# Turning the row maxima of a sliding-window attention on VectorE instead of TensorE, with eight small DMAs per head pair

## The chip, the cores and the metric

The kernel runs on one core of one Trainium2 chip. The metric is the device time of one execution in microseconds (us), the median of the runs given. A difference of 0.2% or less can't be told from no change with this kernel.

## The reference

One transformer block with adaptive layer norm, in fp32: 2048 tokens, width 448, 16 heads of 28, a causal window of 256 keys, and a feed-forward of width 1792 with the Mish activation.

```python
mod = (_silu(c) @ w_mod).reshape(c.shape[0], 6, 1, -1)
sa, ca, ga, sb, cb, gb = (mod[:, i] for i in range(6))
h = _layernorm(x) * (1 + ca) + sa
q, k, v = split(h @ wqkv)                      # 16 heads of 28
scores = einsum("bhqd,bhkd->bhqk", q, k) * 28 ** -0.5
scores = where(0 <= iq - ik < 256, scores, -1e9)
x = x + ga * (softmax(scores) @ v) @ wo
h = _layernorm(x) * (1 + cb) + sb
x = x + gb * (mish(h @ w1 + b1) @ w2)
```

## The kernel before, in words

The tokens are cut into four groups of 512. A group's attention goes head by head, 64 heads over all (`NS`), and each head in three steps `u` (192 steps). A head's queries stand in a tile `q` of 86 rows by 512 tokens, its keys in `k` of 86 rows by 768. fp32 values are carried as a high and a low part, so a head's 28 dimensions take 84 rows. Rows 84 and 85 of `q` hold the high and the low part of each query's row maximum, and the same rows of `k` hold -1: the matmul that makes the scores for the exponential subtracts the maximum as it goes. Two heads share one `q` tile (a "pair", 32 over all); there are three such tiles.

A head passes these steps, and instructions stand in each engine's queue in the order in which the loop over `u` writes them:

- `L` loads `q` and `k` of a head, five heads ahead. Every DMA of this stretch is issued by SP (`dma`, line 59), in program order.
- `A` (lines 676 to 687), three heads ahead: for each of four blocks `t` of 128 queries TensorE makes 128 x 384 scores `sA`, and VectorE adds the mask and reduces them to a maximum per query, a column of `mx`.
- `M2` (lines 689 to 697), once a pair: carries the pair's maxima to the `q` tile. The maxima stand with the queries on 128 partitions (8 columns, head by block), and rows 84 and 85 want them along the free dimension of one partition. `M2` stands three steps `u` ahead of the pair's first `B`.
- `B` (line 713) makes the scores `sB` transposed, keys by queries, for one third of the head; ScalarE takes the exponential twice (`P`, `Ph`), GpSimd makes the low part `Pl`, and `PV` (line 745) multiplies by the values.

Between these, filler matmuls (the projections of the next group, the output projection of the last) are put on TensorE. After the attention comes the feed-forward. TensorE works its queue in order; a waiting `sB` holds whatever stands behind it.

The tile framework makes the waits: an instruction waits for semaphores of those that wrote what it reads. DMAs take turns on eight semaphores, `DMAHW0` to `DMAHW7`.

Of the kernel before, what the change touches and what calls it, by code (L numbers as in the profile page):

```python
# [8 lines left out]
F32 = mybir.dt.float32  # L9
F32R = mybir.dt.float32r  # L10
BF16 = mybir.dt.bfloat16
AF = mybir.ActivationFunctionType
ALU = mybir.AluOpType
# [7 lines left out]
NQ, NK, NV, LEAD = 6, 6, 10, 3  # L21
# [30 lines left out]
def adaln_block(ctx: ExitStack, tc: tile.TileContext, x, wqkv, wo, w1, b1, w2, c, w_mod, out):  # L52
    nc = tc.nc
    PE, ACT, DVE, POOL = nc.tensor, nc.scalar, nc.vector, nc.gpsimd
# [3 lines left out]
    def dma(o, i):  # L58
        nc.sync.dma_start(o, i)

    def pool(name, side="left", space=None):
        kw = {} if space is None else {"space": space}
        cm = tc.tile_pool(name=name, bufs=1, reuse_waits="tile", side=side, **kw)
        st = ExitStack()
        return st.enter_context(cm), st
# [26 lines left out]
    def bank(tag, bufs, name):  # L92
        return PS[0].tile([128, 512], F32, name=name, tag=tag, bufs=bufs)
# [18 lines left out]
    for k in range(4):  # L112
        wmf = st0.tile([128, 2 * D], F32, name=f"wm01_{k}")
        t = wmf[0:112]
# [11 lines left out]
    for part in range(3):  # L126
        for ci in range(4):
            r0, r1 = ci * 128, min(ci * 128 + 128, D)
            for h in ((slice(0, 128),) if ci < 3 else (slice(0, 64), slice(64, 128))):
                t = wqs[ci][h]  # L130
# [9 lines left out]
    ident = cst.tile([128, 128], F32, name="ident")  # L140
# [329 lines left out]
    Q2 = [kq.tile([86, 2, GT], F32R, name="q2_0")]  # L470
# [43 lines left out]
    att, att_s = pool("att")  # L514
# [5 lines left out]
    for i in range(2):  # L520
        t = att.tile([128, GT], F32, name=f"o2_{i}")
# [150 lines left out]
    NS = NG * H  # L672
    mx, Pt, Ph, Pl, pvb, et, olt = {}, {}, {}, {}, {}, {}, {}
    junk = att.tile([128, 384], F32, name="junk")

    def A(i, t):
        g, h = divmod(i, H)
        q, k = Q3[i % NQ], K3[i % NK]
        if i % 2 == 0 and t == 0:
            mx[i // 2] = att.tile([128, 2, 4], F32, name=f"mx{i}", tag="mx", bufs=2)  # L680
        c0 = max(256 - 128 * t, 0) if g == 0 else 0
        p = bank("sA", 2, f"sA{i}_{t}")
        PE.matmul(p[:, c0:384], q[0:84, t * 128:(t + 1) * 128], k[0:84, t * 128 + c0:t * 128 + 384],  # L683
                  start=True, stop=True)
        DVE.tensor_tensor_reduce(out=junk[:, c0:384], in0=p[:, c0:384], in1=mask[:, c0:384], scale=1.0,  # L685
                                 scalar=-3.0e38, op0=ALU.add, op1=ALU.max,
                                 accum_out=mx[i // 2][:, i % 2, t:t + 1])

    def M2(pr):
        p = bank("tr", 1, f"mt{pr}")  # L690
        PE.transpose(p[0:8, 0:128], mx[pr].rearrange("p a t -> p (a t)"), ident)
        r = att.tile([8, 2, 128], F32R, name=f"mr{pr}", tag="mr", bufs=2)
        DVE.tensor_copy(r[:, 0], p[0:8, 0:128])
        DVE.tensor_tensor(r[:, 1], p[0:8, 0:128], r[:, 0].bitcast(F32), op=ALU.subtract)
        for i in range(2):
            dma(Q2[pr % (NQ // 2)][84 + i:85 + i].bitcast(F32).rearrange("o a (t n) -> o (a t) n", t=4),
                r[:, i].bitcast(F32))

    def units(g, b):
        return [x for x in BLOCKS[b] if g > 0 or x[0] >= 2]  # L700
# [324 lines left out]
    for i in range(LEAD):  # L1025
        for t in range(4):
            A(i, t)
            fill0()
            side_step(0)
        if i % 2:  # L1030
            M2(i // 2)
            load_slot(LEAD + 1)
    NU = 3 * NS
    credit = 0.0
    for u in range(NU + 9):
# [14 lines left out]
        a = s + LEAD  # L1050
        if a < NS:
            A(a, (0, 1, 3)[k])
        if k == 0 and (a - 1) % 2 == 1 and LEAD <= a - 1 < NS:
            M2((a - 1) // 2)
        if k == s % 2 and s < NS:
            load_slot(s + LEAD + 2)
        if s % 2 == 1 and 1 <= (s - 1) // 2 <= NS // 2:
            pr = (s - 3) // 2
# [24 lines left out]
        if k == 1 and a < NS:  # L1083
            A(a, 2)
# [73 lines left out]
    for n in range(NN + 1):  # L1158
        g, f = divmod(n, NF)
# [47 lines left out]
```

## Time and profile before

| | before |
|---|---|
| median of 3 runs | 705.66 us (704.79 to 706.11) |
| span of the profiled execution, first to last instruction | 703.9 us |
| what the median has above that span | 1.76 us |
| TensorE clock granted | 1.000 |
| bytes read from and written to HBM | 56.60 MB and 32.51 MB |
| DMA engines' busy share of the span | 42.0% |
| attention with its fillers | 44 to 400 us |

How to read the profile: PE is TensorE, PEld its loading of weights, DVE VectorE, ACT ScalarE, POOL GpSimd and SP SyncE, which here only issues DMAs (SPq is its sequencer, and a row's duration there is the time of the issue, not of the transfer). A row of the timeline has the start and the duration in us, engine, line, operation, and out<-in; in brackets the idle time before it and what ended it. A row of a tile has the shortest, median and longest duration in ns. In a row of waits stand the sum in us, how many, and the longest. The mean in a row of groups is in ns, behind the busy us.

### The profile page before, as it was taken

Reading aid. Unit: us, or ns where it says so; the run is one execution under the profiler, and the core shown is the slowest. Engines: PE = TensorE matmul, PEld = TensorE weight load, DVE = VectorE, ACT = ScalarE, POOL = GpSimd, SP = SyncE. Lnnn points to the kernel's source line nnn. Section 1 sums busy time; section 2 is a strip of 40 time slices with the busy share of each in tenths; the row PEclk is TensorE's granted clock in tenths of the full one; section 3 lists DMA queues with packets and bytes.
Section 4 is the critical chain, followed back from the end, with each engine's and each line's share of the span. In section 5 each row is a group of like instructions: output and inputs, shape, how many; then the busy total and the mean of one; then the engine's idle time right before and its main releaser. Section 6 shows DMA issues by size and latency. Waiting matters only on the chain.

```text
span 703.9 us, 11999 instructions
## 1 busy us (share of the span) xinstructions
PE 685.9 (97%) x4001; PEld 590.2 (84%) x4001; DVE 383.3 (54%) x1030; ACT 391.6 (56%) x740; POOL 326.4 (46%) x355
## 2 busy tenths in 40 slices
PE   9899999999999999999999899999999999999997
PEld 8777888888888888898887788878888888888886
DVE  5688658788655887655768755452224222421112
ACT  3628788777667867667878974344233323332221
POOL 6626779686666776666778957212010000000000
PEclk9999999999999999999999999999999999999999
DMA  7865664455662462663773165800350035001001
GB/s 209 259 221 188 208 204 152 139 181 157 181 209 76 158 207 88 185 211 95 226 216 120 54 203 170 227 20 1 104 117 4 0 106 119 1 1 52 1 1 52
DMA packets 75178, 90.16 MB, mean 128 GB/s; under 512 B 31535, under 2 KB 51741, under 8 KB 75117
## 3 DMA queue, kind: packets, MB, share of 16 engines
q1 hardware_dynamic: 74652, 89.39, 42.0%
q8 instruction: 32, 0.52, 0.3%
q14 instruction: 30, 0.24, 0.1%
q10 hardware_dynamic: 464, 0.00, 0.0%
HBM read 56.60 MB, written 32.51 MB: 127 GB/s over the span
## 4 chain that ended last, share of the span: by engine, by line
PE 78%; DVE 6%; DMA 6%; ACT 3%; POOL 3%; issue 3%; SPq 1%; DVEq 0%; POOLq 0%; ACTq 0%
PE z L917 17%; PE pv L745 10%; PE qk L315 8%; PE sA L683 5%; PE acc L1106 5%; PE acc L1104 5%; PE acc L1105 5%; PE sB L713 5%; PE wo L315 4%; PE qk_v L315 4%; PE sB L724 3%; DMA scr<-st 2%; PE et L759 2%; PE warm L428 1%; DVE junk L685 1%
## 5 line engine op out<-in xcount | busy, mean ns | idle before, releaser
L735 POOL TENSOR_TENSOR Pl<-P,Ph 128x512 fp32r<-128x512 f32 (+2 forms) x192 | 234.8, 1230 | 80.9 <-ACT Ph L728 46.6
L685 DVE CUSTOM_DVE_ANT_0 junk<-sA,mask 128x384 f32<-128x384 f32 (+2 forms) x256 | 135.1, 528 | 95.1 <-PE sA L683 87.4
L727 ACT ACTIVATE P<-sB 128x512 f32<-128x512 f32 (+2 forms) x192 | 109.6, 571 | 62.3 <-PE sB L724 58.1
L925 DVE TENSOR_TENSOR al<-t,ah 128x512 fp32r<-128x512 f32 x56 | 39.2, 700 | 181.8 <-ACT ah L924 181.8
L923 ACT ACTIVATE t<-z,b1c 128x512 f32<-128x512 f32 x56 | 38.3, 684 | 138.6 <-PE z L917 138.6
L728 ACT ACTIVATE Ph<-sB 128x512 fp32r<-128x512 f32 (+2 forms) x192 | 109.2, 569 | 0.0
L683 PE MATMUL sA<-k,q 84*128 84x384 f32 (+2 forms) x256 | 100.5, 396 | 1.8 <-DVE mx L685 1.1
L917 PE MATMUL z<-hlf,w 128*128 128x512 f32 x224 | 88.6, 395 | 0.0
L917 PE MATMUL z<-hhf,w 128*128 128x512 f32 x224 | 88.6, 395 | 0.0
L1104 PE MATMUL acc<-w2h,ah 128*128 128x448 f32 x224 | 82.2, 367 | 1.2 <-ACT ah L924 1.2
L1106 PE MATMUL acc<-w2h,al 128*128 128x448 f32 x224 | 82.1, 366 | 0.1
L1105 PE MATMUL acc<-w2l,ah 128*128 128x448 f32 x224 | 81.6, 364 | 0.0
L745 PE MATMUL pv<-Ph,v 128*60 128x256 f32 (+2 forms) x352 | 76.7, 292 | 0.6 <-ACT o L751 0.5
L745 PE MATMUL pv<-Pl,v 128*60 128x256 f32 (+2 forms) x352 | 74.0, 284 | 2.4 <-POOL Pl L735 1.4
L713 PE MATMUL sB<-q,k 86*128 86x256 f32 (+1 forms) x352 | 74.2, 285 | 0.5 <-DMA q<-mr 0.5
L917 PE MATMUL z<-hhf,w1l 128*128 128x512 f32 x168 | 66.3, 395 | 0.0
L713 PEld LDWEIGHTS sB<-q,k 86*128 86x128 f32 x352 | 61.5, 189 | 2.3 <-DMA q<-mr 1.5
L724 PE MATMUL sB<-fdmask,identr 128*128 128x128 bf16 (+1 forms) x320 | 60.1, 253 | 0.0
L745 PEld LDWEIGHTS pv<-Ph,v 128*60 128x60 f32 x352 | 45.8, 133 | 14.0 <-ACT o L751 1.9
L745 PEld LDWEIGHTS pv<-Pl,v 128*60 128x60 f32 x352 | 45.2, 132 | 11.5 <-POOL Pl L735 3.8
L683 PEld LDWEIGHTS sA<-k,q 84*128 84x128 f32 x256 | 48.9, 193 | 7.0 <-DVE mx L685 4.3
L917 PEld LDWEIGHTS z<-hlf,w 128*128 128x128 f32 x224 | 42.2, 188 | 10.0
(159 smaller groups left out, 1252.4 us busy)
## 6 DMA issues: line engine op xcount, KB each, us to landing
scr<-st SPq DMA_DIRECT2D x24, 512.0 KB
k<-scr SPq DMA_DIRECT2D x48, 252.0 KB
q<-scr SPq DMA_DIRECT2D x64, 168.0 KB
scr<-st SPq DMA_DIRECT2D x32, 256.0 KB
x<-x1d SPq DMA_DIRECT2D x10, 448.0 KB
xin<-in_A_x_dram SPq DMA_DIRECT2D x8, 448.0 KB
xr<-in_A_x_dram SPq DMA_DIRECT2D x16, 224.0 KB
x1d<-xr SPq DMA_DIRECT2D x16, 224.0 KB
```

Of the source, the lines that this page charges most:

```text
L315: PE.matmul(p, b, a, start=(n == 0), stop=(n == 10))
L683: PE.matmul(p[:, c0:384], q[0:84, t * 128:(t + 1) * 128], k[0:84, t * 128 + c0:t * 128 + 384], start=True, stop=True)
L685: DVE.tensor_tensor_reduce(out=junk[:, c0:384], in0=p[:, c0:384], in1=mask[:, c0:384], scale=1.0, scalar=-3.0e38, op0=ALU.add, op1=ALU.max ...
L713: PE.matmul(p[:, c:c + 128 * (t1 - t0)], k[:, jj * 128:(jj + 1) * 128], q[:, t0 * 128:t1 * 128], start=(n == 0), stop=False, skip_group_ch ...
L727: ACT.activation(P[:, c0:], p[:, c0:], AF.Exp, scale=SCALE)
L728: ACT.activation(Ph[u][:, c0:], p[:, c0:], AF.Exp, scale=SCALE)
L735: eng.tensor_tensor(Pl[u][:, a:b], Pt[u][:, a:b], Ph[u][:, a:b].bitcast(F32), op=ALU.subtract)
L745: PE.matmul(pv[0:60, t0 * 128:t1 * 128], V[j % NV][:, h, :], P[u][:, c:c + 128 * (t1 - t0)], start=(P is Ph and b == 0 and n == 0), stop=F ...
L917: PE.matmul(zb[n], ps[m][1], ps[m][0], start=(m == 0), stop=(m == 10))
L1104: PE.matmul(p, ah[n][:, ts], w2h[f], start=(f == 0), stop=False)
L1105: PE.matmul(p, ah[n][:, ts], w2l[f], start=False, stop=False)
L1106: PE.matmul(p, al[n][:, ts], w2h[f], start=False, stop=(f == NF - 1))
```

## The change

Before, TensorE turns the 128 x 8 block of maxima to 8 x 128 in PSUM (`mt`), VectorE splits that in high and low part (`mr`, 8 partitions of 128 tokens each), and two DMAs, one for each part, carry 8 rows of 128 tokens to rows 84 and 85 of the pair's `q`. After, VectorE splits the maxima where they stand (8 columns high, 8 columns low, in the tile `mhl` of 32 columns), turns `mhl` in four blocks of 32 x 32 by one instruction, and finds in `mr`, for each block of 32 tokens, 8 partitions of high and 8 of low parts. Each part of each block goes by a DMA of its own: 2 x 4 of them, 8 rows of 32 tokens each. `mx` becomes a flat tile of 8 columns, and `mhl` is cleared once by GpSimd.

```diff
+    mhl = att.tile([128, 32], F32R, name="mhl")
+    POOL.memset(mhl.bitcast(F32), 0.0)
...
-            mx[i // 2] = att.tile([128, 2, 4], F32, name=f"mx{i}", tag="mx", bufs=2)
+            mx[i // 2] = att.tile([128, 8], F32, name=f"mx{i}", tag="mx", bufs=2)
...
     def M2(pr):
-        p = bank("tr", 1, f"mt{pr}")
-        PE.transpose(p[0:8, 0:128], mx[pr].rearrange("p a t -> p (a t)"), ident)
-        r = att.tile([8, 2, 128], F32R, name=f"mr{pr}", tag="mr", bufs=2)
-        DVE.tensor_copy(r[:, 0], p[0:8, 0:128])
-        DVE.tensor_tensor(r[:, 1], p[0:8, 0:128], r[:, 0].bitcast(F32), op=ALU.subtract)
+        DVE.tensor_copy(mhl[:, 0:8], mx[pr])
+        DVE.tensor_tensor(mhl[:, 8:16], mx[pr], mhl[:, 0:8].bitcast(F32), op=ALU.subtract)
+        r = att.tile([128, 32], F32, name=f"mr{pr}", tag="mr", bufs=2)
+        DVE.transpose(r, mhl.bitcast(F32))
         for i in range(2):
-            dma(Q2[pr % (NQ // 2)][84 + i:85 + i].bitcast(F32).rearrange("o a (t n) -> o (a t) n", t=4),
-                r[:, i].bitcast(F32))
+            rows = Q2[pr % (NQ // 2)][84 + i:85 + i].bitcast(F32).rearrange("o a (t n) -> o (a t) n", t=4)
+            for b in range(0, 128, 32):
+                dma(rows[:, :, b:b + 32], r[b + 8 * i:b + 8 * i + 8])
```

`M2` is called at the same place. What it moves shows in the engines' queues. SP near the end of the attention, before (`q<-mr` is a DMA of the maxima, `q<-scr` and `k<-scr` are loads of a head, `x1d<-xr` is a store):

```order
L59 DMA x1d<-xr_5261 128x448
L59 DMA q_2_460<-mr_5657 1x8x128 x2
L59 DMA q_1_459<-scr 84x512
L59 DMA k_2_146<-scr 84x768
L59 DMA x1d<-xr_5517 128x448
L59 DMA q_1_459<-scr 84x512
L59 DMA k_3_148<-scr 84x768
```

The same place on SP after the change:

```order
L59 DMA x1d<-xr_5398 128x448
L59 DMA q_2_460<-mr_5804 1x8x32 x8
L59 DMA q_1_459<-scr 84x512
L59 DMA k_2_146<-scr 84x768
L59 DMA x1d<-xr_5664 128x448
L59 DMA q_1_459<-scr 84x512
L59 DMA k_3_148<-scr 84x768
```

Nothing changes its place; six more issues stand ahead of the loads that follow. VectorE at a pair's `M2`, before (`ISA` is the masked reduction and the reading of its result into `mx`):

```order
L685 ISA junk,mx_4385<-sA_0_4386,mask 128x384
L685 ISA mx_4385 128x1
L693 CAST mr_4391<-mt_4389 8x128
L694 TENSOR_TENSOR mr_4391<-mt_4389,mr_4391 8x128
L175 SCALAR_TENSOR_TENSOR wm_0_4161<-wm_1_4191,sT,wm_0_4161 112x448
```

and after:

```order
L687 ISA junk,mx_4497<-sA_0_4498,mask 128x384
L687 ISA mx_4497 128x1
L692 CAST mhl<-mx_4315 128x8
L693 TENSOR_TENSOR mhl<-mx_4315,mhl 128x8
L695 STREAM_TRANSPOSE mr_4503<-mhl 128x32
L175 SCALAR_TENSOR_TENSOR wm_0_4268<-wm_1_4298,sT,wm_0_4268 112x448
```

Two instructions become three, in the same place behind the next pair's first reduction. TensorE from a pair's `M2` to the pair's first `sB`, before, with the semaphores that each row waits for (`L315` is filler):

```order
L683 MATMUL sA_0_2358<-k_0_142,q_0_377 128x384 [waits DMAHW7_49,DMAHW6_49,DVE_49]
L691 MATMUL mt_2361<-ident,mx_2168 8x128 [waits DVE_49]
L315 MATMUL wo_1_2333<-wol_472,hho_2111 128x448
...
L713 MATMUL sB_2449<-q_2_460,k_4_150 128x384 [waits DMAHW7_49,DMAHW0_49]
L713 MATMUL sB_2449<-q_2_460,k_4_150 128x128
```

and after:

```order
L685 MATMUL sA_0_2415<-k_0_142,q_0_377 128x384 [waits DMAHW1_49,DMAHW0_49,DVE_49]
L315 MATMUL wo_1_2390<-wol_472,hho_2163 128x448
L315 MATMUL wo_1_2390<-wo_1_468,hlo_2164 128x448
...
L715 MATMUL sB_2511<-q_2_460,k_4_150 128x384 [waits DMAHW4_49,DMAHW5_49,DMAHW3_49,DMAHW6_49,DMAHW2_49,DMAHW7_49,DMAHW1_49,DMAHW0_49]
L715 MATMUL sB_2511<-q_2_460,k_4_150 128x128
```

The transpose `mt` is gone, 32 times in all, and the first `sB` of a pair waits for all eight DMA semaphores in place of two.

More of the change, by code (lines that the diff above doesn't have):

```diff
@@ L686, in A @@
                                  scalar=-3.0e38, op0=ALU.add, op1=ALU.max,
-                                 accum_out=mx[i // 2][:, i % 2, t:t + 1])
+                                 accum_out=mx[i // 2][:, i % 2 * 4 + t:i % 2 * 4 + t + 1])
     def M2(pr):
-        p = bank("tr", 1, f"mt{pr}")
-        PE.transpose(p[0:8, 0:128], mx[pr].rearrange("p a t -> p (a t)"), ident)
-        r = att.tile([8, 2, 128], F32R, name=f"mr{pr}", tag="mr", bufs=2)
-        DVE.tensor_copy(r[:, 0], p[0:8, 0:128])
-        DVE.tensor_tensor(r[:, 1], p[0:8, 0:128], r[:, 0].bitcast(F32), op=ALU.subtract)
+        DVE.tensor_copy(mhl[:, 0:8], mx[pr])
+        DVE.tensor_tensor(mhl[:, 8:16], mx[pr], mhl[:, 0:8].bitcast(F32), op=ALU.subtract)
+        r = att.tile([128, 32], F32, name=f"mr{pr}", tag="mr", bufs=2)
+        DVE.transpose(r, mhl.bitcast(F32))
         for i in range(2):
-            dma(Q2[pr % (NQ // 2)][84 + i:85 + i].bitcast(F32).rearrange("o a (t n) -> o (a t) n", t=4),
-                r[:, i].bitcast(F32))
+            rows = Q2[pr % (NQ // 2)][84 + i:85 + i].bitcast(F32).rearrange("o a (t n) -> o (a t) n", t=4)
+            for b in range(0, 128, 32):
+                dma(rows[:, :, b:b + 32], r[b + 8 * i:b + 8 * i + 8])
     def units(g, b):
```

## The prediction

> **What bounds the kernel now.** I read the page first, then the stretch in which the changed code runs (44 to 400 us), then the rows of the tiles that the change touches.
>
> ```profile
> PE 685.9 (97%) x4001; PEld 590.2 (84%) x4001; DVE 383.3 (54%) x1030; ACT 391.6 (56%) x740; POOL 326.4 (46%) x355
> ...
> PEclk9999999999999999999999999999999999999999
> ...
> PE 78%; DVE 6%; DMA 6%; ACT 3%; POOL 3%; issue 3%; SPq 1%; DVEq 0%; POOLq 0%; ACTq 0%
> ```
>
> TensorE is busy 97% of the span at full clock, and 78% of the chain that ended last is TensorE's. By stage:
>
> ```profile
> 44.00:400.00 356.00, 348.52 (x2386) 299.09 (x2385) 254.21 (x793) 267.00 (x538) 256.29 (x242) 1.00 0.53 165
> ```
>
> In the attention stretch (columns: span, then PE, PEld, DVE, ACT, POOL busy) PE is busy 348.5 of 356 us; no other engine is over 267. So a new PE wait here counts in full, and a DVE instruction counts only if PE ends up waiting for it. The whole `mr` path today:
>
> ```profile
> L59 SPq DMA_DIRECT2D q<-mr x64: 625/640/1362, 44.8 to 396.4; - x64
> L693 DVE CAST mr<-mt x32: 272/274/279, 44.5 to 395.3; 8x128 fp32r<-8x128 f32 x32
> L694 DVE TENSOR_TENSOR mr<-mt,mr x32: 277/279/280, 44.8 to 395.7; 8x128 fp32r<-8x128 f32 x32
> ```
>
> The number to keep is 640 ns: SP spends that to issue one `q<-mr` DMA, and nothing else passes SP meanwhile. One head pair in order of time (pair 17 of 0 to 31):
>
> ```profile
> 229.66 0.42 PE L683 MATMUL sA<-k,q 84*128 84x384 f32 x1
> 229.92 0.27 PE L691 MATMUL mt<-ident,mx 128*8 128x128 f32 x1
> ...
> 230.12 0.56 DVE L685 CUSTOM_DVE_ANT_0 junk<-sA,mask 128x384 f32<-128x384 f32 x1
> ...
> 230.60 0.27 DVE L693 CAST mr<-mt 8x128 fp32r<-8x128 f32 x1
> ...
> 230.90 1.38 SPq L59 DMA_DIRECT2D q<-mr  x2
> 230.91 0.28 DVE L694 TENSOR_TENSOR mr<-mt,mr 8x128 fp32r<-8x128 f32 x1
> ```
> ```profile
> 235.57 0.37 PEld L713 LDWEIGHTS sB<-q,k 86*128 86x128 f32 x2
> ```
>
> The last row is the pair's first score tile, which reads rows 84 and 85 of `q` and so needs every `mr` DMA. From first issue to use: 235.57 - 230.90 = 4.67 us. I call this D. It differs from pair to pair; the first pair, the longest and the last:
>
> ```profile
> 44.83 2.17 SPq L59 DMA_DIRECT2D q<-mr  x2
> ...
> 48.23 0.19 PEld L713 LDWEIGHTS sB<-q,k 86*128 86x128 f32 x1 [0.80 <-DMA q<-mr]
> ```
> ```profile
> 204.46 1.51 SPq L59 DMA_DIRECT2D q<-mr  x2
> ```
> ```profile
> 210.57 0.36 PEld L713 LDWEIGHTS sB<-q,k 86*128 86x128 f32 x2
> ```
> ```profile
> 395.64 1.35 SPq L59 DMA_DIRECT2D q<-mr  x2
> ```
> ```profile
> 398.23 0.30 PEld L713 LDWEIGHTS sB<-q,k 86*128 86x128 f32 x2
> ```
>
> D is 3.40, 6.11 and 2.59 us; over all 32 pairs the same two rows give 3.98 on the mean. In the first pair PE already waited for the landing:
>
> ```profile
> 45.64 2.49 DMA q<-mr
> ```
> ```profile
> PEld sB L713 <- DMA q<-mr: 1.5, 3, 0.8
> ```
>
> The second DMA landed at 45.64 + 2.49 = 48.13, and SP had finished issuing at 44.83 + 2.17 = 47.00: landing comes 1.13 us after the last issue ends. Three such waits cost 1.5 us in the whole run; today the path just fits.
>
> **Part by part. The PE transposes (32, removed).** On the chain one of them takes:
>
> ```profile
> 52.73 0.11 PE mt L691
> ```
>
> 32 x 0.11 = 3.5 us of PE time. PE also waited for the maxima before some of them:
>
> ```profile
> PEld mt L691 <- DVE mx L685: 2.3, 3, 0.9
> ```
>
> That makes 5.8 us, the most this can give. But the transpose stands in the stretch between `M2` and the score tile. If that stretch ends in a wait for DMAs, PE merely arrives earlier at the wait, so in the forecast I count it as nothing.
>
> **DVE: two instructions become three.** Before, the first DMA went 0.30 us after the first of them began (230.60 to 230.90), beside the second. Now both DMA halves need the turned block. The nearest rows:
>
> ```profile
> L414 DVE TENSOR_SCALAR sT<-sT 112x4 f32<-112x4 f32 x1 | 0.1, 136 | 0.0
> ```
> ```profile
> L416 DVE TENSOR_TENSOR sT<-sT,cT 112x4 f32<-112x4 f32 x1 | 0.2, 164 | 0.0
> ```
> ```profile
> L1139 DVE STREAM_TRANSPOSE zt<-z 128x512 f32<-128x512 f32 x12 | 8.4, 704 | 0.0
> ```
> ```profile
> L685 DVE CUSTOM_DVE_ANT_0 junk<-sA,mask 128x384 f32<-128x384 f32 x224 | 123.9, 553 | 80.2 <-PE sA L683 76.1
> ...
> L685 DVE CUSTOM_DVE_ANT_0 junk<-sA,mask 128x128 f32<-128x128 f32 x16 | 4.6, 287 | 11.9 <-PE sA L683 8.5 <-issue 3.2
> ```
>
> 256 columns more cost 553 - 287 = 266 ns, 1.04 ns each, so a 32-column transpose should take about 704 - 480 x 1.04 = 205 ns (bounds 136 and 704). 0.14 + 0.16 + 0.21 = 0.51 us, then the issue: the first DMA goes 0.22 us later. DVE's total stays as it is (0.51 against 0.55 a pair). It no longer waits for PE here, but the row of line 685 above (230.12, just ahead of the cast) shows that the previous reduction, not the transpose, ended last; nothing is gained. The one POOL memset lies in the setup and costs nothing.
>
> **SP: two issues become eight.** Two take 1.38 us, so start to start is 0.74, and eight take 7 x 0.74 + 0.64 = 5.82 us. The new form, 8 pieces of 128 B for 8 of 512 B, isn't in the trace. Bounds, from a load's issue and from eight DMAs in a row:
>
> ```profile
> L59 SPq DMA_DIRECT2D q<-scr x64: 308/408/1236, 30.9 to 379.2; - x64
> ```
> ```profile
> 446.59 4.37 SPq L59 DMA_DIRECT2D z<-xnd  x8
> ```
>
> At 0.31 and the 0.10 gap of the `mr` row, eight would take 3.2 us; as the `z` loads 4.37; at the first pair's 2.17 for two, 8.7. I take 5.82: same source and target, same number of pieces; only the length of a piece changes, and 2 KB rows issue faster than these, so length isn't what costs.
>
> A sentence of the Trainium skill speaks against this. "DMA: Bandwidth & Descriptors", section "Anatomy of one DMA", puts sequencer dispatch at about 50 ns and the rest of a fixed 2.0 us in the completion; by it (an estimate, for a path told there of GpSimd) eight issues would end in 0.4 us, all landed 2.4 us after the first, inside every D but not more. The 640 ns row disagrees by more than ten times, so the sum goes by the row.
>
> **The sum.** Delay 0.22 + issues 5.82 + landing 1.13 = 7.17 us, against D = 3.98: PE waits 3.19 us a pair, x 32 = 102 us. Queued behind the waiting score tile are, in PE's order, its masks, the next `sA`, the filler matmuls and all `pv`; ACT, DVE and POOL run dry behind them, so no one makes it up. What comes back are small waits in these 356 us that a pause lets drain, such as
>
> ```profile
> PEld qk L315 <- PE sA L683: 2.0, 2, 1.0
> ...
> PE qk L315 <- DVE hl L262: 1.5, 2, 0.8
> ```
>
> All of PE's rows there together are about 20 us, half outside the stretch that is hidden anyway; I take 6. So +96: 703.9 + 96 = 799.9 by this execution's span. The median of the runs, 705.66, stands 1.76 above the span, so 801.7; I say **801**.
>
> **What SP holds up behind them.** The six more issues move each later load by 5.82 - 1.38 = 4.44 us:
>
> ```profile
> 232.38 0.90 SPq L59 DMA_DIRECT2D scr<-st  x2
> 233.37 0.80 SPq L59 DMA_DIRECT2D q<-scr  x1
> 236.17 0.32 SPq L59 DMA_DIRECT2D k<-scr  x1
> ...
> 243.34 1.40 SPq L59 DMA_DIRECT2D q<-mr  x2
> ```
>
> This `q` and `k` serve the `sA` that runs 1.24 us ahead of the next `mr` issue (230.90 - 229.66 in the pair above), so at 242.10. Moved, `k` issues at 240.61 and lands, with the 2.49 us of a landing, near 243.1; but `sA` itself moves to 245.3. Covered by the new wait, without which it would be late by 1 us. In the stage with most stores SP is fuller, so a few us more are possible, up to 1 us in each of the first ten pairs.
>
> **Rivals.** B: the new form issues faster. Eight in 4.37 us make 5.72 against 3.98: 1.74 x 32 - 6 = +50, 755; eight in 3.2 make 4.55: 0.57 x 32 = 18, +3 for the two pairs with D of 6.11 that give nothing back, -6: +15, 721. For it speaks only that most DMAs on SP are cheaper.
>
> C: the granted clock falls after each wait. The trace shows 1.00 and no long idle, so neither way. If PE ran at half clock for as long as it had waited, it would lose half of 3.19 us each time, 51 more: 852. The Trainium skill, "TensorE: Matmul & The Clock Gate", section "Why this matters for your kernels", warns of PE gaps over about 3 us; no run here yet shows it, and by it only the longer waits would count (an estimate: the 13 pairs with D under 3.8, some 20 us).
>
> D, the other side: everything lands in time, and the transposes' 5.8 us are gained: 699.9. It decides at 8 issues in 3.98 - 0.22 - 1.13 = 2.63 us for the mean pair, 0.33 each, and 0.15 each for the last pair. The fastest issue in the rows above is 0.31 plus a gap.
>
> E: no difference, where B's cheapest price and the saved transposes cancel.
>
> **Chances.** Forecast 0.72 (its own range 775 to 835, from late loads above and faster issues below), B 0.15, C 0.07, D 0.04, E 0.02. The range 735 to 840 leaves out D, E, the cheap half of B and C: some 0.2. Faster by over 0.2% (about what can be told here from no change) 0.04, within 0.2% 0.02, slower 0.94.
>
> **What would show it.** `q<-mr` on SP 256 times at about 640 ns and some 5.8 us per eight; "PEld sB <- DMA q<-mr" rising from 1.5 to about 100 us in 32 waits; PE's share of the span near 86%; the attention stretch longer by about 96 us and the feed-forward unchanged; `STREAM_TRANSPOSE` near 205 ns; clock 1.00. I am wrong if the issue takes 0.3 us, or if the wait appears under another name (`sA` for late loads).

## The result and the profile after

| | before | after |
|---|---|---|
| median of 4 runs | 705.51 us (704.79 to 706.11) | 870.29 us (865.62 to 873.91) |
| span of the profiled execution | 703.9 us | 863.8 us (its time 865.62) |
| TensorE clock granted, mean | 1.000 | 0.923 |

After against before is 1.2326 (95% interval 1.2271 to 1.2381): 165 us slower, where 95 were forecast. First the page of after, engines, granted clock and chain:

```profile
PE 739.9 (86%) x3969; PEld 629.4 (73%) x3969; DVE 403.4 (47%) x1062; ACT 393.4 (46%) x740; POOL 323.9 (37%) x356
...
PEclk9987887889899999899988989699999999999999
...
PE 55%; SPq 18%; DMA 10%; DVE 9%; issue 5%; ACT 2%; DVEq 0%; POOL 0%; ACTq 0%; POOLq 0%
```

SP's sequencer has gone from 1% to 18% of the chain that ended last, and the landing of DMAs from 6% to 10%: the path the forecast named. The middle line it did not forecast: the clock dips all through the attention. TensorE's busy time is 54 us more than before with 32 instructions fewer. By stage (columns: span, then PE, PEld, DVE, ACT, POOL busy, clock, DMA share, GB/s):

```profile
44.00:130.00 86.00, 59.62 (x303) 46.27 (x303) 41.56 (x132) 37.42 (x83) 31.93 (x35) 0.80 0.34 110
...
400.00:560.00 160.00, 124.78 (x746) 106.84 (x745) 85.14 (x249) 86.75 (x170) 83.97 (x76) 0.87 0.38 114
560.00:863.00 303.00, 298.92 (x1407) 257.90 (x1405) 100.19 (x168) 106.06 (x170) 45.18 (x52) 1.00 0.24 70
```

The attention now lasts to 560 us instead of 400; the feed-forward has its 303 us as before. All 160 us of span are in the attention. The tiles `mr` and `mhl` of after (shortest, median, longest in ns):

```profile
L59 SPq DMA_DIRECT2D q<-mr x256: 620/632/761, 44.8 to 556.2; - x128
L695 DVE STREAM_TRANSPOSE mr<-mhl x32: 211/211/214, 44.6 to 551.2; 128x32 f32<-128x32 f32 x32
```
```profile
L692 DVE CAST mhl<-mx x32: 166/435/1171, 44.1 to 549.8; 128x8 fp32r<-128x8 f32 x32
L693 DVE TENSOR_TENSOR mhl<-mx,mhl x32: 166/168/1220, 44.3 to 550.8; 128x8 fp32r<-128x8 f32 x32
```

A piece of 128 B costs SP what one of 512 B did, 632 ns against 640. The transpose is at its price too. But an instruction on 8 columns takes 166 ns or up to seven times that. Then after's waits, the sum in us, how many, and the longest:

```profile
PEld sB L715 <- issue: 72.5, 20, 6.2
PE sB L715 <- DMA k<-scr: 50.1, 16, 5.9
PE sB L715 <- DMA q<-mr: 42.9, 13, 5.2
...
PEld sA L685 <- DVE mx L687: 15.8, 16, 2.8
...
PE sA L685 <- DVE mx L687: 11.9, 12, 2.5
```

The row of before that answers to the first of the last two (the other stood at 1.1 us):

```profile
PEld sA L683 <- DVE mx L685: 4.3, 12, 0.6
```

PE waits for the landing in about 30 pairs. The row named `k<-scr` is a wait of the same kind: the loads share the eight semaphores with the `mr` DMAs, and in the timeline these waits too end behind the last `mr` piece: in all 32 pairs the `sB` runs 1.06 to 1.63 us after the last issue ends. The waits of `sA` for the reductions, 4.3 us before, have grown too. One pair in order of time:

```profile
190.69 0.42 PE L685 MATMUL sA<-k,q 84*128 84x384 f32 x1
...
191.63 0.17 DVE L692 CAST mhl<-mx 128x8 fp32r<-128x8 f32 x1
...
191.83 0.17 DVE L693 TENSOR_TENSOR mhl<-mx,mhl 128x8 fp32r<-128x8 f32 x1
...
192.23 0.21 DVE L695 STREAM_TRANSPOSE mr<-mhl 128x32 f32<-128x32 f32 x1 [0.24 <-DVE mhl L693]
...
192.47 5.34 SPq L59 DMA_DIRECT2D q<-mr  x8
...
193.02 0.40 PE L715 MATMUL sB<-q,k 86*128 86x256 f32 x2
...
196.38 0.40 PE L747 MATMUL pv<-Pl,v 128*60 128x128 f32 x2
...
199.07 0.47 PE L715 MATMUL sB<-q,k 86*128 86x384 f32 x2 [2.29 <-DMA q<-mr]
...
201.87 0.63 PE L715 MATMUL sB<-q,k 86*128 86x256 f32 x2
```

Eight issues end at 197.81; the `sB` runs at 199.07, 1.26 us later, and PE stood still for 2.29 us. Then the same form of `sB` that took 0.40 us at 193.02 takes 0.63 at 201.87. The windows around it show what lies between:

```profile
196.31:199.72 3.41, 1.12 (x9) 0.80 (x8) 0.91 (x4) 0.57 (x2) 1.26 (x1) 1.00 0.27 102
199.72:203.14 3.42, 3.42 (x15) 2.84 (x14) 1.34 (x5) 2.24 (x5) 1.67 (x3) 0.50 0.72 209
203.14:206.55 3.41, 3.08 (x27) 2.62 (x25) 3.04 (x10) 3.36 (x7) 3.25 (x5) 1.00 0.80 259
```

In the first PE was busy 1.12 of 3.41 us; in the next the granted clock is 0.50 and PE is busy throughout; then it is back. Over the trace of after PE runs 133 us at half clock, 114 of them in work; before, 0.4 us.

To say where the time goes in all pairs, I cut each into four stretches and took means over pairs 1 to 30 from the timelines (us), for this kernel and for those of the experiments below. The last `sA` is the one ahead of the pair's `mr` issue in the program, the next pair's first, and counts from its start; the period goes from one pair's first issue to the next one's:

| kernel | last `sA` to first `mr` issue | first issue to end of last | end of last to first `sB` | `sB` to next pair's last `sA` | period | half clock in all |
|---|---|---|---|---|---|---|
| before | 1.30 | 1.40 | 2.82 | 5.89 | 11.46 | 0.4 |
| after | 2.36 | 5.41 | 1.30 | 7.31 | 16.37 | 133 |
| pe8 | 1.32 | 5.54 | 1.33 | 6.86 | 15.05 | 84 |
| pe8fill | 1.36 | 5.53 | 1.48 | 5.97 | 14.37 | 5 |
| pe6 | 1.29 | 4.17 | 1.26 | 6.44 | 13.19 | 39 |
| pe4 | 1.33 | 2.80 | 1.70 | 5.90 | 11.76 | 1 |
| dve2 | 2.42 | 1.35 | 2.36 | 5.94 | 12.10 | 7 |
| dve2ps | 1.87 | 1.36 | 2.36 | 5.88 | 11.53 | 5 |
| mxps | 1.97 | 5.46 | 1.31 | 7.59 | 16.35 | 143 |
| fill26 | 2.45 | 5.51 | 1.68 | 6.06 | 15.69 | 17 |

The table is made from one profiled execution each, which for after is the shortest of its four (865.62 us) and for mxps the longest (862.65), so small differences between those two rows may be chance.

After less before: 1.06 + 4.01 - 1.52 + 1.42 = 4.97 us a pair, x 32 = 159; the spans differ by 160. So three suspects: eight issues, a later first issue, and slower work behind the wait. The experiments part them.

### The profile page after: what moved, and what is told of

It is laid out like the page before. It is cut to its first block, busy times and chain, and to the rows that moved or that the text cites. A ratio compares the mean times of both kernels' runs of the same rounds, so it can differ in the third digit from the quotient of the medians.

```text
span 863.8 us, 12268 instructions
## 1 busy us (share of the span) xinstructions
PE 739.9 (86%) x3969; PEld 629.4 (73%) x3969; DVE 403.4 (47%) x1062; ACT 393.4 (46%) x740; POOL 323.9 (37%) x356
## 4 chain that ended last, share of the span: by engine, by line
PE 55%; SPq 18%; DMA 10%; DVE 9%; issue 5%; ACT 2%; DVEq 0%; POOL 0%; ACTq 0%; POOLq 0%
SPq L59 18%; PE z L919 15%; PE acc L1108 5%; PE acc L1106 5%; PE acc L1107 5%; PE pv L747 5%; PE qk L315 5%; PE sB L715 4%; PE sA L685 3%; DMA scr<-st 3%; DMA q<-mr 3%; DVE junk L687 3%; PE wo L315 2%; PE sB L726 2%; PE qk_v L315 2%
## 5 line engine op out<-in xcount | busy, mean ns | idle before, releaser
L715 PE MATMUL sB<-q,k 86*128 86x256 f32 (+1 forms) x352 | 85.5, 320 | 99.7 <-DMA k<-scr 50.1
L715 PEld LDWEIGHTS sB<-q,k 86*128 86x128 f32 x352 | 68.6, 216 | 108.8 <-issue 72.5
L685 PE MATMUL sA<-k,q 84*128 84x384 f32 (+2 forms) x256 | 109.9, 434 | 12.3 <-DVE mx L687 11.9
L747 PE MATMUL pv<-Ph,v 128*60 128x256 f32 (+2 forms) x352 | 83.2, 313 | 0.5 <-ACT o L753 0.3
L747 PE MATMUL pv<-Pl,v 128*60 128x256 f32 (+2 forms) x352 | 79.5, 301 | 0.1
L685 PEld LDWEIGHTS sA<-k,q 84*128 84x128 f32 x256 | 55.6, 220 | 18.9 <-DVE mx L687 15.8
L726 PE MATMUL sB<-fdmask,identr 128*128 128x128 bf16 (+1 forms) x320 | 66.2, 275 | 0.0
L747 PEld LDWEIGHTS pv<-Ph,v 128*60 128x60 f32 x352 | 50.8, 147 | 16.2 <-issue 2.2
L747 PEld LDWEIGHTS pv<-Pl,v 128*60 128x60 f32 x352 | 49.8, 144 | 9.6 <-issue 1.2
L753 ACT ACTIVATE o<-pv 60x512 f32<-60x512 f32 x61 | 36.0, 590 | 31.4 <-PE pv L747 31.0
```

What stands on the lines that cost most here:

```text
L715: PE.matmul(p[:, c:c + 128 * (t1 - t0)], k[:, jj * 128:(jj + 1) * 128], q[:, t0 * 128:t1 * 128], start=(n == 0), stop=False, skip_group_ch ...
L747: PE.matmul(pv[0:60, t0 * 128:t1 * 128], V[j % NV][:, h, :], P[u][:, c:c + 128 * (t1 - t0)], start=(P is Ph and b == 0 and n == 0), stop=F ...
```

## The experiments

All ratios are against the kernel before on the same chip, whose median was 705.2 to 705.5 us.

**The eight DMAs alone (pe8).** Before's transpose on TensorE stays; only its two DMAs become eight.

```diff
-            dma(Q2[...][84 + i:85 + i]....rearrange("o a (t n) -> o (a t) n", t=4), r[:, i]...)
+            rows = Q2[...][84 + i:85 + i]....rearrange("o a (t n) -> o (a t) n", t=4)
+            for c in range(0, 128, 32):
+                dma(rows[:, :, c:c + 32], r[:, i, c:c + 32].bitcast(F32))
```

> The kernel before, TensorE transpose kept, but each of its two DMAs split in four of 8 x 32 (the DMAs alone, without the VectorE part). Theory 1 (the eight issues on SP are the cause): like the changed kernel, 855 to 885, clock 0.91 to 0.94. Rival (the VectorE path or its place makes the wait): 705 to 715.

829.29 us (824.23 to 833.03), ratio 1.1776 (1.1733 to 1.1819), below the 855 to 885 expected. Of the 165 us, about 124 are the DMAs' and about 41 hang on the VectorE path, more than expected; the runs of pe8 alone spread over 9 us. Of pe8's tile `mr`, and its cores:

```profile
L59 SPq DMA_DIRECT2D q<-mr x256: 625/634/1227, 44.9 to 514.9; - x128
```
```profile
core 0: 822.4 us, clock 0.949
```

**The same with PE kept busy (pe8fill).** pe8 with 20 matmuls that nothing reads, put ahead of each pair's first `sB` into the bank that this `sB` overwrites. They wait for no DMA, so they run in the pause.

```diff
         p = bank("sB", 2, ...)
+        if u % 6 == 0:
+            for _ in range(20):
+                PE.matmul(p[:, 0:256], identr, fdmask, start=True, stop=True, skip_group_check=True)
```

> TensorE transpose with eight DMAs, and 20 extra matmuls (2.1 us) ahead of each pair's first score tile, inside waits of 1.6 to 4.7 us. Theory (in the run with eight DMAs alone, 124 us are 32 x 2.7 us of lateness and 32 x about 1 us of half clock in the work after it): the time from that tile to the next sA falls from 6.86 to about 6.0 us, half clock from 83 us to under 20, and the time by 25 to 32 us, to 797 to 806. Rival (the clock costs nothing, the stretch after the tile is longer for another reason, as late loads): 825 to 835.

802.22 us (800.6 to 806.99), ratio 1.1377 (1.1335 to 1.1418): with more work it is 27 us faster than pe8. Cores, then the attention's windows up to 400 us:

```profile
core 0: 799.3 us, clock 0.997
```
```profile
44.00:400.00 356.00, 337.35 (x2386) 286.38 (x2384) 199.06 (x630) 207.94 (x422) 197.38 (x189) 1.00 0.43 133
```

The clock is 1.00 and the `sB` stretch is back at 5.97 us (before 5.89, pe8 6.86). So the clock is 27 of pe8's 124 us, or some 5 more, since the filling itself delays `sB` by 0.15 us a pair (1.48 against 1.33), and the eight issues are 97 or some 5 less. The forecast's +96 is near this, but holds 7 us (0.22 x 32) for the VectorE path; its terms for the issues alone give 89. So part of the closeness is luck.

**Six and four DMAs (pe6, pe4).** The same edit with pieces of 48, 48 and 32 tokens, or of 64.

> TensorE transpose with six DMAs (48, 48 and 32 tokens of each block). Theory (lateness beyond D, and a clock that falls only where a pause fills most of 3.41 us): 5 x 0.69 + 0.63 + 1.32 = 5.4 us against a D of 3.98 on the mean, 47 us of waits, and 5 to 10 us of clock, because most waits are under 2 us: 750 to 765. Rival (every DMA beyond two costs the same 20.7 us): 785 to 792.

pe6: 762.09 us (761.1 to 766.23), ratio 1.0808 (1.0773 to 1.0843), clock 0.975. The time is in the expected range, in part by luck: the stretch behind `sB` is 0.55 us a pair longer than before, 18 us in all at 39 us of half clock, where 5 to 10 us were expected of the clock.

> The kernel before with four DMAs of 8 x 64 in place of two. Theory 1 (a wait begins only where the last landing comes after the tile is due): 4 x 0.69 + 1.13 = 3.9 us against D of 2.6 to 6.1 us, so 13 pairs wait 0.2 to 1.3 us, 8 us in all, and no clock falls: 708 to 716. Rival (each extra DMA costs the same, a third of the change's 165 us): 750 to 765.

pe4: 716.79 us (716.23 to 718.12), ratio 1.0166 (1.0151 to 1.0182), clock 0.999, just above the expected range. Its tile `mr`:

```profile
L59 SPq DMA_DIRECT2D q<-mr x128: 620/634/1463, 45.4 to 408.1; - x128
```

Pieces of 256 B cost 634 ns as well: the price is per DMA. Each two more DMAs lengthen the issue by 1.37 to 1.40 us a pair; the time went +12 (4 DMAs), +57 (6), +124 (8). The slack holds most of the first step; behind it each step costs up to 44 us of issue (1.37 x 32) and what the clock adds.

**The VectorE path alone (dve2).** After, with only the first two of the eight DMAs; the rows that get no maxima stand at zero, and the exponential is scaled down so that it stays finite.

```diff
-            for b in range(0, 128, 32):
+            for b in (0,):
...
+        POOL.memset(t[64:86].bitcast(F32), 0.0)
...
-        ACT.activation(P[:, c0:], p[:, c0:], AF.Exp, scale=SCALE)
+        ACT.activation(P[:, c0:], p[:, c0:], AF.Exp, scale=SCALE / 32)
```

> The VectorE path alone: split and turn as in the change, but only the two DMAs of the first 32 tokens of each block (the other six are left out, the rows start as zeros, and the exponential's scale is divided by 32, so the output is not the reference's). Theory 1 (eight issues make the waits, the VectorE path only adds about 1.1 us between the last sA and the first issue): 1.06 + 1.4 + 1.2 us after a first issue due at 1.30 stays inside D for nearly all pairs, clock 1.00, 700 to 715. Rival (the VectorE path costs 40 us by itself, as the difference between the changed kernel and the run with the DMAs alone): 735 to 750.

726.06 us (725.12 to 729.5), ratio 1.0306 (1.0284 to 1.0329), between the two theories, with the clock at 0.995. So the path costs 21 us without any extra DMA. In the table its first `mr` issue comes 1.12 us later than before, and dve2's waits show PE held at `sA`, whose banks the delayed reductions free:

```profile
PEld sA L689 <- DVE mx L691: 19.0, 20, 2.8
PE sA L689 <- DVE mx L691: 14.0, 12, 2.6
```

What is slow is the cast or the subtraction, whichever comes while GpSimd works, mostly at `Pl`. In the trace of after 21 casts and 10 subtractions took over 200 ns; all 31 began while a GpSimd instruction ran (29 times `Pl`) and ended 18 to 35 ns after its end, and none of the 33 quick ones lies wholly inside a GpSimd instruction. The transpose is not held: 30 of its 32 overlap a GpSimd instruction, at 211 to 214 ns. The timeline of after at another pair, where GpSimd makes three `Pl` in a row:

```profile
171.00 2.94 POOL L737 TENSOR_TENSOR Pl<-P,Ph 128x512 fp32r<-128x512 f32 x3 [0.74 <-PE pv L747]
...
171.92 0.39 DVE L692 CAST mhl<-mx 128x8 fp32r<-128x8 f32 x1
...
172.35 0.93 DVE L693 TENSOR_TENSOR mhl<-mx,mhl 128x8 fp32r<-128x8 f32 x1
...
173.31 0.21 DVE L695 STREAM_TRANSPOSE mr<-mhl 128x32 f32<-128x32 f32 x1
```

**The maxima through PSUM (mxps, dve2ps).** VectorE first copies `mx` to PSUM, so that neither the cast nor the subtraction has more than one input in SBUF or runs from SBUF to SBUF; one instruction more.

```diff
+        p = bank("tr", 1, f"mt{pr}")
+        DVE.tensor_copy(p[:, 0:8], mx[pr])
-        DVE.tensor_copy(mhl[:, 0:8], mx[pr])
-        DVE.tensor_tensor(mhl[:, 8:16], mx[pr], mhl[:, 0:8].bitcast(F32), op=ALU.subtract)
+        DVE.tensor_copy(mhl[:, 0:8], p[:, 0:8])
+        DVE.tensor_tensor(mhl[:, 8:16], p[:, 0:8], mhl[:, 0:8].bitcast(F32), op=ALU.subtract)
```

First in after (mxps), then in dve2 (dve2ps).

> The changed kernel with the maxima first copied to PSUM, so that the split's cast and subtraction read PSUM and no VectorE instruction of it has two SBUF operands or copies SBUF to SBUF; one small instruction more. Theory 2 (cast and subtraction wait for GpSimd's 1.28 us instruction at the SBUF port that the two engines share): all of them take 0.16 to 0.28 us each time, sA to first issue falls from 2.36 to about 1.75 us, and the time to 835 to 852. Rival (they wait for their data or for the reduction's end): maxima of about 1.2 us stay, 870 to 880.

857.31 us (856.58 to 862.65), ratio 1.2169 (1.2141 to 1.2197). Its tile `mhl`:

```profile
L694 DVE CAST mhl<-mt x32: 166/166/169, 44.0 to 546.8; 128x8 fp32r<-128x8 f32 x32
L695 DVE TENSOR_TENSOR mhl<-mt,mhl x32: 166/166/167, 44.2 to 547.0; 128x8 fp32r<-128x8 f32 x32
```

The slow ones are gone from all 64. The time fell by 13 us only, less than expected: the first issue comes 0.39 us earlier (12 us over 32 pairs), and no more was gained behind it. In the profiled execution the work behind the wait even costs 0.28 us more a pair (half clock 143 us), but that is the longest of the four, at a clock of 0.917 against 0.926 in the others.

> The VectorE path alone (two DMAs, as before: the other six left out, rows start as zeros, the exponential's scale divided by 32, output not the reference's), with the maxima taken through PSUM first. Theory (of the 20 us that the path alone cost, most come from cast and subtraction waiting at the port that VectorE shares with GpSimd, and the reductions queued behind them): sA to first issue about 1.9 us, waits of sA for the reductions fall from 33 to about 12 us, and the time from 726 to 708 to 716. Rival (it is the number of small instructions): 722 to 730.

708.02 us (706.05 to 709.01), ratio 1.0031 (1.0017 to 1.0045). Of the 21 us of the VectorE path about 18 (726.06 - 708.02) were the collision with GpSimd; with it gone, turning the maxima on VectorE costs 2.8 us with the clock up and two DMAs. The waits of dve2ps at `sA`, which were 19.0 and 14.0:

```profile
PEld sA L689 <- DVE mx L691: 9.1, 16, 1.9
...
PE sA L689 <- DVE mx L691: 4.7, 6, 1.7
```

**After with PE kept busy (fill26, fill13).** After, with 26 or 13 such matmuls ahead of each pair's first `sB`.

> The changed kernel with 26 extra matmuls of 256 columns (about 26 x 0.107 = 2.8 us of TensorE) ahead of each pair's first score tile, into the same PSUM bank, which is then overwritten. They run while the tile waits for the eight DMAs, whose wait is 2.3 to 5.9 us. Theory 1 (two costs: about 106 us of waits, and about 57 us because the clock falls to half in and after them): the clock stays at 0.99 or more, and the time falls by 50 to 60 us, to 805 to 820. Rival (the clock is only a sign, the time is all waiting): 865 to 880, or more by the extra matmuls.

843.38 us (835.18 to 844.13), ratio 1.1932 (1.1876 to 1.1988). The clock came back to 0.990, and the stretch behind `sB` from 7.31 to 6.06 us a pair, 40 us over 32 pairs; but the time fell by 27 us, not by 50 to 60. A row of the waits of fill26 (after had 42.9, 13, 5.2):

```profile
PE sB L718 <- DMA q<-mr: 10.6, 10, 2.3
```

Some waits are shorter than the filling, which then delays `sB`: end of the last issue to `sB` is 1.68 us in place of 1.30 (12 us over the pairs), and the first issue and its seven followers come 0.19 us later (6 us). 40 - 12 - 6 = 22 us, by which the two profiled spans differ (863.8 and 841.8).

> The same with 13 extra matmuls (1.4 us): 1.0 to 3 us of each wait stay idle. Theory 1, if the clock falls only where a stretch of 3.41 us is mostly idle: the clock stays above 0.98 and the time is 810 to 825. Rival (any pause of about 1 us lowers the clock): clock 0.92 to 0.95 and 840 to 870.

847.41 us (844.07 to 848.48), ratio 1.2007 (1.198 to 1.2035), clock 0.967, 55 us at half: half the filling saves part of the falls, with the clock between the two theories and the time in the rival's range. The estimate of 50 to 60 us had taken half of all 114 us of slow work, though the stretch behind `sB` had grown by 45 us only, and had put the filling at nothing. Why the stretch grew by less than half of the slow work in it (about 99 us in pairs 0 to 29) is not shown.

**Half of the issues on another queue (twoq).** After, with the four DMAs of the low parts issued by ScalarE.

```diff
-                dma(rows[:, :, b:b + 32], r[b + 8 * i:b + 8 * i + 8])
+                (nc.sync, nc.scalar)[i].dma_start(rows[:, :, b:b + 32], r[b + 8 * i:b + 8 * i + 8])
```

> The changed kernel with the four DMAs of the low parts issued by ScalarE's queue, the four of the high parts by SP. Theory 1 (it is the serial issue on one queue): four issues take 2.7 us, the last landing comes about 2.7 us sooner, waits fall to about 0.5 us a pair and the clock stays near 1: 720 to 745. Rival (the DMAs themselves are slow, 8 pieces of 128 B on the same engines): no change, 855 to 875. Second rival: ScalarE is held behind its DMAs (it waits for VectorE and issues for 2.6 us a pair) and the exponentials come late: 750 to 800.

810.47 us (808.79 to 816.19), ratio 1.1503 (1.1471 to 1.1534). The time is outside all three expected ranges, nearest to that of the held ScalarE (750 to 800). First issue to end of last falls from 5.41 to 3.00 us, but the waits of twoq show new ones:

```profile
PE pv L747 <- ACT o L753: 47.4, 26, 4.7
ACT P L729 <- DMA q<-mr: 45.9, 11, 5.5
```

ScalarE stands at its DMA issue, its exponentials and `o` behind that, and PE waits for `o`.

**The maxima earlier (lead4_after, and lead4_before as control).** `M2` one head further ahead of its use (`LEAD` 4 for 3), which the number of `q` and `k` buffers allows only with the loads one head ahead of theirs in place of two. The two runs differ in one more thing: in lead4_after `M2` stands six steps `u` ahead of its pair's first `B`, in lead4_before it is called at a head's third step and stands four ahead (before: three).

> The changed kernel with the maxima made four heads ahead in place of three, so that the eight DMAs have six steps (about 11 us) instead of three before their first use; loads of a head stay five heads ahead and stand before the eight issues. Theory 1 (only the lateness of the last landing counts): no wait for q<-mr, clock 1.00, the transposes saved: 698 to 712. Rival (SP itself is full, later loads and stores come late): 730 to 800.

819.43 us (815.4 to 823.01), ratio 1.1615 (1.1583 to 1.1646).

> The control of the run with maxima made four heads ahead: the kernel before with that lead (the transfer of the maxima one and a third heads ahead, two DMAs). Theory (the 114 us of the run with eight DMAs and that lead came from loads of k and q standing behind eight issues on SP): 703 to 720. Rival (they came from the lead itself, with loads only one head ahead of their use): 770 to 815.

770.99 us (769.71 to 771.99), ratio 1.0922 (1.09 to 1.0944). The lead, with the later loads that it brings, costs before 66 us, at a clock of 0.96. The waits, first of lead4_after, then of lead4_before:

```profile
PE sA L685 <- DMA k<-scr: 60.9, 19, 8.0
```
```profile
PE sA L683 <- DMA k<-scr: 30.0, 14, 4.0
```

No wait of `sB` for `q<-mr` is left in either; late loads have taken its place. So this pair, whose `M2` does not even stand at the same step, tells nothing clean of what eight issues cost a kernel that has time for them; a longer lead with loads as early as before was not tried.

## Why the prediction was wrong

It had the sign, the place and the main mechanism, and nearly its size for that mechanism. It was low by 69 us, and two steps failed: the clock, which the sum puts at nothing ("neither way") and which measured 45 us; and the later first issue, which it has at 0.22 us a pair and which measured 1.06, 27 us more over 32 pairs.

- **Eight issues: right.** Forecast 5.82 us in all, measured 5.41 (0.63 each, 0.05 between), because the 0.10 us gap of the two-DMA row lies between the high and the low part: in pe8 the gap at that place is 0.099 us too (median), and the six others are 0.045. Landing 1.30 us instead of 1.13. Together 6.71 against 6.95. "DMA: Bandwidth & Descriptors" of the Trainium skill, section "Anatomy of one DMA", has 50 ns of dispatch, told there of GpSimd's path; the 632 ns row stands, and so does the choice to go by it. PE stood still 100 us in all ahead of the pairs' first `sB`, where 102 were forecast. Rival B needed 0.31 to 0.55 us an issue and is out.
- **The DVE delay: the mis-sized term.** Forecast 0.22 us a pair, measured 1.06, or 27 us more over 32 pairs. The step that failed is "0.14 + 0.16 + 0.21 = 0.51 us": it took the prices of the cast and the subtraction from two instructions of the setup that GpSimd did not hold, looked at durations and not at what else touches SBUF at that moment, and left out the gaps between the three instructions. Before, both read PSUM and were always 272 to 280 ns. After, they have a mean of 534 and 414 ns, the 166 and 166 of mxps plus 0.62 us; the gaps behind the three (means 0.03, 0.15 and 0.03 us) add another 0.21. These two make up nearly all of the 0.84 us that were missing. The transpose was at its price. Without the collision mxps and dve2ps still start 0.57 to 0.67 us late, with one instruction more. The Trainium skill, "SBUF — State Buffer", section "Who interferes with whom", says it: a DVE instruction with two SBUF inputs contends with a GpSimd instruction that reads SBUF, a copy or cast can contend when it enters a two-port mode, and one with at most one SBUF input outside those modes does not; whichever comes second is blocked. The trace agrees with this for the 31 slow instructions above, and dve2 and dve2ps agree, with about 18 us between them. That the cast was in a two-port mode no row shows.
- **DVE and `sA`: an overlooked consequence.** "A DVE instruction counts only if PE ends up waiting for it" was put down, and then not followed: the delayed reductions hold PE at `sA`, 15.8 and 11.9 us in after's two rows for `mx`.
- **The clock, the term put at nothing: rival C was the case, at a chance of 0.07.** Rival C had +51 us for it; measured +1.42 us a pair, 45 us, in the stretch behind `sB`, of which fill26 gives back 40 with the clock up, and on pe8 alone 27 by pe8fill. Its rule (as long at half clock as PE had waited) was near in size: 108.6 us of pauses over 1 us, 114 us of slow work. What failed is the weight: a before with no pauses can't show what a pause does, and "neither way" should not have become 0.07. "TensorE: Matmul & The Clock Gate" of the Trainium skill was read as speaking of gaps over about 3 us only; the fall after 2.29 us of standing still shows that this is too high a bound for this kernel.
- **The late loads** were small, as put down: after's waits at `sA` have 0.4 us of PE for `k<-scr` and 0.8 of PEld for `q<-scr`. Whether the 6 us came back is not shown; they would lie in the same stretch as the clock's 45.
- **The sum again with measured terms:** (1.06 + 4.01 - 1.52) x 32 = 114, and 1.42 x 32 = 45: 159 against 160 of span. Parted by runs, each to within some 5 us: eight issues 97, their clock 27, VectorE path 41. The path costs 21 alone with two DMAs. That the other 20 come where its delay meets a wait that nothing hides any more is argued, not tested: after less pe8 has 1.04 us a pair in the first stretch and 0.45 behind `sB`.

## What to carry to other kernels

Count DMAs, not bytes: on one queue each costs its issue (0.63 us here for a DMA of eight pieces, of 128 to 512 B alike), and a wait on the path grows by that as soon as the slack between issue and use is gone. Price a forecast stall on TensorE with the clock that follows it, and ask for each VectorE instruction that moves from PSUM to SBUF operands what GpSimd does at that moment. When an experiment keeps TensorE busy with filler work, count what the filler itself costs: in fill26 40 us came back behind the waits, and some 18 were lost again where the filler outlasted the wait and the first issues came later.

## What the runs showed of the hardware

- **The granted clock goes by stretches of 3.41 us on a fixed grid.** In seven traces (after, pe8, pe6, fill13, fill26, mxps, twoq) 117 of 118 falls to 0.50 followed a stretch in which PE was busy for 55% or less (the other 66%); of 1323 stretches at full clock from 40 us on with no fall behind them none was under 41% busy, and 21 were under 55%, so the two groups overlap. It comes back after a stretch that was at least 92% busy, one or two later (in lead4_after, where PE waits longer, up to six later). So 1.5 to 2 us of standing still (45% to 59% of 3.41) within one stretch can do it. "TensorE: Matmul & The Clock Gate" of the Trainium skill, section "What's actually happening", states the same window and that it runs freely, but calls for an idle window; here a half-idle one did it, and the measurement decides. What exactly is counted stays open.
- **A tiny VectorE instruction can take seven times its price** beside GpSimd: 128x8 from 166 to 1220 ns, until the GpSimd instruction ends. `STREAM_TRANSPOSE` of 128x32 never did (211 to 214 ns).
- **The length of a piece does not matter to SP** in these DMAs of eight pieces: 632, 634 and 640 ns (medians) for 128, 256 and 512 B.
